# Key columns reordered by TensorE's reads instead of VectorE's writes, product turns of two engines fixed by waits, and a new written order, in a linear-attention and MLP kernel

## The chip, the cores and the metric

One core of one Trainium2 chip. The time is device microseconds (us) of one execution of the whole program; the kernel before has a median of 96.13 us over four runs.

## What is computed

Four batches b, four heads h, 1088 positions s, head size 32, sketch size r = 8:

```
a1 = S1 x, a2 = S2 x           for x = each row of q and of k      (8 numbers each)
phi(x) = outer(a1, a2)         64 numbers
kv = sum_s phi(k_s) v_s^T      (64 x 32),   z = sum_s phi(k_s)
attn_s = (phi(q_s) . kv) / (phi(q_s) . z + 1e-6)
x = attn, heads side by side   4352 tokens x 128
out = silu(x w_in) w_out       w_in 128 x 2048, w_out 2048 x 128
```

Inputs and output are float32.

## The kernel before

The MLP is cut into groups. An "h" group (L729) makes 1024 columns of x w_in in one of two double PSUM banks ("h" slots, tile H); a silu (L733, ACT) turns it into bf16 tile G; an "o" group (L746, or L743 where tokens are the rows) multiplies G by w_out and accumulates in PSUM. There are 68 groups of each kind. MLP calls are named m00, m02, m04 (batch 0), m10, m14, m20, m24 (batches 1 and 2), mR (the last 64 columns of all batches together), m30, m34, m36 (batch 3); m04h2 is the third h group of m04, m04s2 its silu, m04o2 its o group. Results leave through a transpose (tr) or copies (cp) and stores (st).

The attention for each batch feeds x to these calls. Keys: load (lk1 for batch 1), two VectorE block transposes (kt0 and kt2, function `kt`, L305) into KT, a projection on TensorE (`pairs`, L273: eight float32 matmuls of 64 x 32, one for each of two head pairs p and four column groups c), transposes back into kab (k1tr0, k1tr1, L322), products kp = outer (L328, on VectorE or GpSimd, in parts of two 32-row blocks), z (L334) and l2 (L343, L350) for the denominator's weights wm, kv (L384; in batch 0 L363), its mask copy kvm (L374, or a cast), transpose kvt (L394), copy kvc. Queries: load (lq), transposes (q1tr: L554, L622, L624), projection (L273 in batch 0, L630 after it), transposes back (L576, L581, L640, L641), then prod, red, rec, norm on VectorE (L476, L479, L482, L485), products qp = outer (L495 in batch 0, L649 after it), a transpose of qp by TensorE and a copy (pet, petc) or by DMA (dmat, L655), num (L526, L661), x copies (L163 on ACT, L165 on VectorE and GpSimd).

In KT the columns of a key block are wanted in the order of v's rows. Before, the transposes write them so: for each of four column groups c the elements land at a step of four, `(t s c)` with c innermost, and the projection reads a contiguous slice.

The order of work is not found by the compiler. Every step is a numbered task with its engine (or a choice of engines), a cost that stands only for planning, its dependencies and its slots in PSUM; the string ORDER lists all 484 tasks, "38.1" meaning task 38 on the second of its engines. `emit` walks the string and issues each task; each engine then runs its own tasks in exactly this order and waits by semaphores where data or a slot is not ready. `replay` computes planned times with the costs (it also hands out the slots); before the first h group TensorE is filled with matmuls on a zero tile (L879). SyncE issues the loads, the DMA transposes and most stores in the order of the string. A load waits until its buffer (two of each kind) is free.

The four loads of w_in and w_out halves and quarters (lwi0, lwi1, lwo0 to lwo3) come in float32 and are cast to bf16 in eight tasks cwi0 to cwi3 and cwo0 to cwo3, on GpSimd, ACT or VectorE. Task names carry the batch and first block: q0outer44 is the product of blocks 4 and 5 of batch 0's queries.

Of the kernel before, what the change touches and what calls it, by code (L numbers as in the profile page):

```python
# [16 lines left out]
0 7 22 28 23 1 29 24 2.1 25 33 3.0 30 80 32 8 34 106 31 35 38.1 11 5 40.0 36 14 37 6 55 16 50 111  # L17
48.1 56 51 18 42.0 52 58 20 26.0 59 107 53 27.0 44.0 57 108 81 109 49 110 60 39 61 43 70 46.0 152
62 82 63 9.0 153 64 41 71 65.0 47 154 45 155 4 72 54.1 66 73 156 74 84 67.0 75.1 157 85 83 114 10.1
68 86 12.0 69.0 87 76 88 244 113 77.0 15.0 247 245 89 13.0 78 198 90 115 91.0 248 250 79.1 96.1 92  # L20
116 251 259 117 246 93.1 260 118.0 123 131 262 124 97 119.0 263 125 94 98.1 253 126.0 17.2 95.0
19.0 132 254 120.0 99 133 249 21.1 134 265 112.0 100.0 136 252 266 135 274 137 261 199 275 138 277
255 139 278 264 140 280 141.0 276 281 268 279 143.1 256 142 269 159 267 283 160 282 284 286 177 161
122.0 144 287 121.0 289 163 270 290 162 257 292 206 127 167.0 293 258 271 169 128.0 295 166.0 170
129 273 285 296 130.0 205 171 145.1 147 272 288 165.0 149.1 150.0 291 200 172.0 301 164.0 201 178
202 302 203 168.0 294 179 158.0 328 180 297 181 329 331 298 207 332 182 300 304 183 330 305 184 307
299 209 333 185 308 334 186 303 335 189.0 310 306 311 313 208 190 309 187.0 314 337 336 338 210.0
223 188 316 215 317 214.0 319 146 339 211.0 216 320 322 173 323 217 340 174.0 218.0 175 312 341
176.0 213.1 343 193 191.1 344 346 196.1 204.0 342 347 195.1 349 345 101.1 350 224 315 225 382 226
348 227 383 355 228 351 356 102 385 352 384 386 103.1 388 353 229 357 230 389 148 354 358 231 387  # L30
232 359 391 192 235.0 390 392 394 237.0 318 236 151.1 233.1 395 321 361 393 238 362 364 324 212.0
365 234 367 360 368 104 370 105.1 325 363 371 373 326 396 374 397 219 327 398 400 220.0 366 401 221
376 222.0 369 377 194 240 403 197.1 243.1 399 404 436 239 437 439 241.1 402 440 242.1 442 405 443
409 406 372 410 375 408 412 378 413 407 415 379 438 416 445 381 411 446 418 380 414 419 452 417 453
421 441 422 455 444 456 424 447 425 427 448.1 449.1 420 428 451.0 430 423 431 426 450.0 468 454 469
471 429 472 458 457 459 461 432 462 474 433 460 475 477 435 463 478 470 465.1 434 473 464.1 466.1
476 467.0 479 481.1 480.0 482.1 483.0
# [9 lines left out]
class Plan:  # L47
# [3 lines left out]
    OTHER, MODE, FREE = 0.17, 0.09, 0.2  # L51
# [25 lines left out]
    def replay(self, seq):  # L77
        now, mode, queue, port = dict(self.now), None, 4.3, 0.0
        free = {k: [(i, 0.0) for i in range(len(v))] for k, v in self.slots.items()}
        for t, c in seq:  # L80
            eng, cost = t["eng"][c], t["cost"][c]
            at = max(now.get(eng, 0.0), t["ready"])
            for d in t["deps"]:
                at = max(at, d["end"] if d["dq"] and t["dq"] else d["done"] + d["lag"] + self.hop(d["on"], eng) * (d["dq"] == 0.0))
            got = []
            for pool in t["take"]:
                i, when = free[pool].pop(0)
                got.append(i)
                at = max(at, when)
            if eng == "PE":  # L90
                cost += self.MODE if mode not in (None, t["mode"]) else 0.0
                mode = t["mode"]
            if t["tt"] and eng in ("DVE", "POOL"):
                at = max(at, port)
                port = at + cost
            t["on"], t["start"], t["end"], t["got"] = eng, at, at + cost, got
            now[eng] = t["done"] = t["end"]
            if t["dq"]:
                queue = t["done"] = max(queue, t["end"]) + t["dq"]
            for u, i in t["give"]:  # L100
                free[u["take"][i]].append((u["got"][i], t["end"] + self.FREE))

    def emit(self, text, handles, fill, until):
        seq = self.order(text)
        self.replay(seq)
        last = 0.0
        for t, c in seq:
            if t["on"] == "PE":
                if last < until():
                    fill(last, min(t["start"], until()))  # L110
                last = t["end"]
            if t["fn"] is None:
                continue
            args = [self.slots[p][i] for p, i in zip(t["take"], t["got"])]
            if len(t["eng"]) > 1:
                args = [handles[t["on"]]] + args
            t["fn"](*args)
# [3 lines left out]
def kernel(  # L121
# [147 lines left out]
    def pairs(dst, srcT, lo, hi, groups=range(4)):  # L269

        for c in groups:
            for p in range(2):
                nc.tensor.matmul(dst[p][32 * c: 32 * (c + 1), lo:hi], WPf[64 * p: 64 * (p + 1), :],  # L273
                                 srcT[64 * p: 64 * (p + 1), c, lo:hi],
                                 start=True, stop=True, tile_position=(64 * p, 32 * c))

    def load(b):
        def lk():
            Kx[b] = tile_x(b, "Kx")
            load_x(nc.sync, Kx[b], k, b, 0, SA)  # L280

        def lq():
            Qx[b] = tile_x(b, "Qx")
            load_x(nc.sync, Qx[b], q, b, 0, SA)
        dk = dq = ()
        if b >= 2:
            dk, dq = ks[b - 2]["kt"], qs[b - 2]["tr"]
        at = (6.2, 24.0, 43.0)[b - 1]
        ks[b]["lk"] = dma(557, lk, dk, due=at, name=f"lk{b}")
        dv = ks[b - 2]["vcs"] if b >= 2 else []  # L290
        ks[b]["lv"] = [dma(139, lambda c=c: load_v(nc.sync, b, c), dv, due=at + 0.5, name=f"lv{b}{c}") for c in range(4)]
        qs[b]["lq"] = dma(557, lq, dq, due=at + 1.0, name=f"lq{b}")

    def key_tasks(b, cuts):
# [6 lines left out]
        def kt(c, lo, hi):  # L301
            hi = min(hi, KN[c])
            src = Kx[b][:, KA[c]: KA[c + 2], :].rearrange("p (c a) d -> p c a d", c=2)[:, :, lo:hi, :]
            dst = KT.rearrange("p q (t s c) -> p c t q s", s=8, c=4)[:, c:c + 2, lo:hi]
            nc.vector.transpose(out=dst, in_=src.rearrange("p c a d -> p c (a d)"))  # L305

        def proj0(lo, hi):
            st["p", lo] = [(H1 if lo else H0)[:, i, 0:CW] for i in range(2)]
            pairs(st["p", lo], KT, 32 * lo, 32 * hi)

        def proj(s0, s1):
            st["p", 0] = [s0, s1]
            pairs(st["p", 0], KT, 0, CW)
# [11 lines left out]
        def outer(eng, lo, hi):  # L325
            a = st["ab"][:, 0, lo:hi, :].rearrange("p a (h r) -> p (a h) r", h=H)
            bb = st["ab"][:, 1, lo:hi, :].rearrange("p a (h r) -> p (a h) r", h=H)
            eng.tensor_tensor(out=st["kp"][:, H * lo: H * hi], in0=_bc(a, 2, R), in1=_bc(bb, 1, R), op=ALU.mult)  # L328
# [75 lines left out]
        if b == 0:  # L404
            lv = [dma(139, lambda c=c: load_v(nc.sync, 0, c), due=5.0 + 0.1 * c, name=f"lv0{c}") for c in range(4)]
# [9 lines left out]
        for i, (lo, hi) in enumerate(parts):  # L415
# [6 lines left out]
            if b == 0:  # L422
                pr = pl.add("PE", 0.09 + 0.055 * (hi - lo), lambda lo=lo, hi=hi: proj0(lo, hi), k1 + [wts["WP"]] + st["pr"],
# [21 lines left out]
        tz = pl.add("PE", 0.36, z, st["tr"], take=("s",), mode="32", name=nm("z"))  # L445
# [18 lines left out]
    def scale_tasks(b, aq, mq, g0, n, deps, nm):  # L464
# [9 lines left out]
        def prod():  # L474
            alloc()
            nc.vector.tensor_tensor(out=AW[b % 2][:, g, 0:R], in0=aq(), in1=mq(), op=ALU.mult)  # L476
# [7 lines left out]
        def norm():  # L484
            nc.vector.tensor_tensor(out=st["aqs"][:, g], in0=aq(), in1=_bc(st["den"][:, g], 1, R), op=ALU.mult)  # L485
# [6 lines left out]
    def outers(b, eng, bq, lo, hi):  # L492
        st = qs[b]
        st[f"qp{lo}"] = work.tile([P, (hi - lo) * H, R, R], BF16, name="qp", tag=f"qp{lo}")
        eng.tensor_tensor(out=st[f"qp{lo}"], in0=_bc(st["aqs"][:, H * lo: H * hi], 2, R),  # L495
# [47 lines left out]
    def query_tasks(b, spans, pe=False, groups=None):  # L543
# [17 lines left out]
        def proj(s0=None, s1=None):  # L561
            st["p", lo0] = [H1[:, 0], H1[:, 1]] if first else [s0, s1]
            pairs(st["p", lo0], QT, 32 * lo0, 32 * hi0)
# [20 lines left out]
        def outer(eng, lo, hi):  # L584
            outers(b, eng, st["abm"][:, 1, lo:hi], lo, hi)
# [4 lines left out]
        pr = pl.add("PE", 0.09 + 0.058 * nn, proj, [t] + (kst["tr"][2:4] if first else []), take=() if first else ("s", "s"),  # L590
# [23 lines left out]
    def query_tasks_hm(b):  # L614
# [31 lines left out]
        def outer(eng, i):  # L646
            g0, n = (2 * NB * i, 2 * NB) if i < 2 else (H * NB, H)
            st["qp", i] = work.tile([P, n, R, R], BF16, name="qp", tag=f"hp{i}")
            eng.tensor_tensor(out=st["qp", i], in0=_bc(st["aqs"][:, g0: g0 + n], 2, R),  # L649
# [166 lines left out]
    def wq():  # L816
        for w in WQ:
            nc.gpsimd.tensor_tensor(out=w[:, 0: 2 * R].rearrange("p (n r) -> p n r", n=2), in0=WP[:, :, 0, :], in1=WP[:, :, 1, :], op=ALU.add)
# [5 lines left out]
    ld_qa = dma(262, lambda: load_x(nc.sync, Qx[0], q, 0, 0, 16), due=4.0, rate=280.0, name="lqa")  # L824
# [13 lines left out]
    for i in range(2):  # L838
        t = dma(524, lambda i=i: load_in(i), due=8.0 + 0.1 * i, rate=350.0, name=f"lwi{i}")
        win += [pl.add(("POOL", "ACT", "DVE"), (0.66, 0.6, 0.6), lambda e, w=w: cast_w(e, w_in, w_inf, w), [t], name=f"cwi{w}")  # L840
                for w in (2 * i, 2 * i + 1)]
    for i in range(4):
        t = dma(262, lambda i=i: load_out(i), due=9.0 + 0.1 * i, rate=320.0, name=f"lwo{i}")
# [8 lines left out]
    qs[0]["lq"] = dma(300, lambda: load_x(nc.sync, Qx[0], q, 0, 16, SA), due=6.0, name="lqb")  # L852
# [28 lines left out]
    pl.emit(ORDER, {"ACT": nc.scalar, "DVE": nc.vector, "POOL": nc.gpsimd, "SP": nc.sync}, fill, lambda: first_h[0]["start"])  # L881
# [30 lines left out]
```

## Time and profile before

| | |
|---|---|
| median of four runs (lowest, highest) | 96.13 us (95.72, 96.62) |
| the profiled execution | 96.6 us, span of the instructions 94.5 us |
| PE, ACT, DVE, POOL busy | 85.7, 72.9, 57.1, 37.2 us |
| first h group; last matmul ends | 16.58 us; 90.43 us |
| ACT silus | 68, 1042 ns each, next one 915 ns after the start |
| TensorE clock | full in all slices |

PE is TensorE, DVE VectorE, ACT ScalarE, POOL GpSimd, SP SyncE. A row of instructions gives start, length, engine, line, operation, what it writes and reads, its shape and how many; in brackets stands the idle time before it and who released it. In the group rows the numbers after the bar are busy us in all, mean ns of one, idle time before. A transpose or silu overlaps the next one's start, so start-to-start distances are shorter than the lengths. Before 7 us TensorE's matmuls take about double the later time per column.

### The profile page before, as it was taken

The page shows a single profiled execution, that of the slowest core. Times are in us where ns is not written, and L with a number is a line of the kernel's source. Part 1 is how long each engine was busy: PE and PEld are TensorE (multiplying, and loading weights), DVE is VectorE, ACT ScalarE, POOL GpSimd, SP SyncE. Part 2 cuts the span into 40 slices and gives each one's busy share as a digit, 9 for nine tenths or more (in the row PEclk, how much of TensorE's full clock was granted, in tenths as well). Part 3 has the DMA queues.
Part 4 walks back from the last instruction along what each step waited for, and adds up shares of the span by engine and source line. Part 5 has one row for each costly group of instructions (what it writes and reads, how often), then busy time and mean ns, then how long its engine had stood idle before and what let it go on. Part 6 is the DMA issues. An engine that isn't in the chain of part 4 may idle for free.

```text
span 94.5 us, 2456 instructions
## 1 busy us (share of the span) xinstructions
PE 85.7 (91%) x954; PEld 48.8 (52%) x954; DVE 57.1 (60%) x151; ACT 72.9 (77%) x92; POOL 37.2 (39%) x48
## 2 busy tenths in 40 slices
PE   5999758699999799999999999999999999999920
PEld 4535434567776253434453354444455667578920
DVE  5689599998789988599917389943227300202210
ACT  2335226969989795599999879999999999999810
POOL 5019508879909879900898000970000000000000
PEclk9999999999999999999999999999999999999999
DMA  1978899999961853596570003464800571010461
GB/s 34 249 240 254 239 383 401 361 326 287 274 256 31 169 96 57 134 299 111 104 146 0 7 0 59 80 132 88 139 12 0 80 116 26 20 41 2 70 125 28
DMA packets 28506, 12.93 MB, mean 137 GB/s; under 512 B 23120, under 2 KB 26704, under 8 KB 28496
## 3 DMA queue, kind: packets, MB, share of 16 engines
q1 hardware_dynamic: 28096, 12.65, 51.9%
q10 hardware_dynamic: 400, 0.14, 0.6%
q8 instruction: 7, 0.11, 0.5%
q14 instruction: 3, 0.02, 0.1%
HBM read 8.79 MB, written 2.23 MB: 117 GB/s over the span
## 4 chain that ended last, share of the span: by engine, by line
PE 64%; DVE 16%; DMA 11%; SPq 3%; issue 1%; DVEq 0%
PE H L729 29%; PE B L746 21%; DMA Kx<-in_k_dram 11%; DVE KT L305 6%; PE B L743 6%; SPq L191 2%; PE H L630 2%; DVE qabm L640 2%; PE B L273 1%; DVE qp L649 1%; PE B L661 1%; DVE QT L622 1%; DVE den L479 1%; DVE AW L476 1%; PE B L384 1%
## 5 line engine op out<-in xcount | busy, mean ns | idle before, releaser
L733 ACT ACTIVATE G<-H 128x1024 bf16<-128x1024 f32 x68 | 64.4, 1042 | 5.8 <-PE H L729 5.3
L729 PE MATMUL H<-xT,w_in 128*128 128x512 bf16 (+1 forms) x160 | 38.2, 337 | 0.0
L746 PE MATMUL B<-G,w_out 128*128 128x512 bf16 (+1 forms) x128 | 32.4, 352 | 0.0
L729 PEld LDWEIGHTS <-w_in 128*128 128x128 bf16 x176 | 18.3, 114 | 11.7 <-issue 4.2
L328 POOL TENSOR_TENSOR kp<-kab 128x512 bf16<-128x512 f32 (+1 forms) x18 | 18.3, 1041 | 11.1 <-DVE kab L322 11.1
L746 PEld LDWEIGHTS <-w_out 128*128 128x128 bf16 x128 | 12.1, 97 | 10.4 <-issue 1.2
L649 POOL TENSOR_TENSOR qp<-aqs,qabm 128x1024 bf16<-128x1024 f32 (+1 forms) x4 | 7.2, 1810 | 9.7 <-DVE aqs L485 9.7
L305 DVE STREAM_TRANSPOSE KT<-Kx 128x512 f32<-128x512 f32 (+4 forms) x10 | 9.3, 957 | 1.0 <-DMA Kx<-in_k_dram 1.0
L751 DVE STREAM_TRANSPOSE ot<-B 128x512 f32<-128x512 f32 (+1 forms) x8 | 5.1, 640 | 7.7 <-PE B L746 7.7
L879 PE MATMUL B<-zero 128*128 128x256 bf16 x36 | 8.0, 356 | 1.1 <-DVE fmask L234 1.1
L649 DVE TENSOR_TENSOR qp<-aqs,qabm 128x1024 bf16<-128x1024 f32 (+1 forms) x5 | 6.9, 1406 | 0.1
L743 PE MATMUL B<-w_out,G 128*128 128x128 bf16 x96 | 6.7, 219 | 0.0
L743 PEld LDWEIGHTS <-G 128*128 128x128 bf16 x96 | 6.0, 98 | 0.7
L165 DVE COPY ot<-B 128x128 f32<-128x128 f32 x5 | 1.3, 287 | 8.0 <-PE B L743 8.0
L879 PEld LDWEIGHTS <-zero 128*128 128x128 bf16 x36 | 4.0, 124 | 2.7 <-DVE fmask L234 1.1
L640 DVE STREAM_TRANSPOSE qabm<-H 128x256 f32<-128x256 f32 x6 | 2.6, 429 | 3.9 <-PE B L630 3.9
L165 DVE CAST xT<-B 128x512 bf16<-128x512 f32 (+1 forms) x6 | 3.7, 640 | 1.8 <-PE B L661 1.8
L495 POOL TENSOR_TENSOR qp<-aqs,qabm 128x512 bf16<-128x512 f32 (+1 forms) x3 | 3.7, 1239 | 0.4 <-DVE aqs L485 0.4
L622 DVE STREAM_TRANSPOSE QT<-Qx 128x1024 f32<-128x1024 f32 x3 | 3.7, 1223 | 0.0
L165 POOL CAST w_in<-w_inf 128x512 bf16<-128x512 f32 x3 | 2.0, 666 | 4.2 <-DMA w_inf<-in_moe_w_in_dram 4.2
L165 POOL CAST Vh<-Vf 128x1152 bf16<-128x1152 f32 x3 | 3.4, 1146 | 0.0
L273 PE MATMUL B<-KT,WP 64*32 64x288 f32 x48 | 2.2, 415 | 1.3 <-DVE KT L305 1.3
(97 smaller groups left out, 77.5 us busy)
## 6 DMA issues: line engine op xcount, KB each, us to landing
Kx<-in_k_dram SPq DMA_DIRECT2D x3, 544.0 KB, 7.3
Qx<-in_q_dram SPq DMA_DIRECT2D x3, 544.0 KB, 5.5
out_dram<-ot SPq DMA_DIRECT2D x24, 64.0 KB, 2.0
Vf<-in_v_dram SPq DMA_DIRECT2D x8, 144.0 KB, 4.4
Vf<-in_v_dram SPq DMA_DIRECT2D x8, 128.0 KB, 4.3
w_inf<-in_moe_w_in_dram SPq DMA_DIRECT2D x2, 512.0 KB, 8.3
w_outf<-in_moe_w_out_dram SPq DMA_DIRECT2D x4, 256.0 KB, 9.0
out_dram<-ot SPq DMA_DIRECT2D x16, 32.0 KB, 1.7
```

The costliest lines, as they stand in the source:

```text
L165: eng.tensor_copy(out=out, in_=in_)
L305: nc.vector.transpose(out=dst, in_=src.rearrange("p c a d -> p c (a d)"))
L328: eng.tensor_tensor(out=st["kp"][:, H * lo: H * hi], in0=_bc(a, 2, R), in1=_bc(bb, 1, R), op=ALU.mult)
L622: nc.vector.transpose(out=QT[:, :, 0: 32 * NB].rearrange("p c (a s) -> p a c s", s=32), in_=Qx[b][:, 0: 4 * NB, :].rearrange("p (a c) d -> ...
L640: nc.vector.transpose(out=dst, in_=st["p"][h][:, 0:NM])
L649: eng.tensor_tensor(out=st["qp", i], in0=_bc(st["aqs"][:, g0: g0 + n], 2, R), in1=_bc(grp(1)[:, g0: g0 + n], 1, R), op=ALU.mult)
L729: nc.tensor.matmul(view(sl, i), w_inj[:, (J * jp + i) // 4, (J * jp + i) % 4, :], x, start=True, stop=True)
L733: nc.scalar.activation(out=sl, in_=cc[jp], func=ACT.Silu)
L743: nc.tensor.matmul(d[:, 0:P], view(cc["g", jp], i)[:, P * t: P * (t + 1)], w_out[:, j, :], start=(j == 0), stop=(j == NJ - 1))
L746: nc.tensor.matmul(cc["o"][:, :n], w_out[:, j, :], view(cc["g", jp], i), start=(j == 0), stop=(j == NJ - 1))
L751: nc.vector.transpose(out=cc["ot"][:, :n], in_=cc["o"][:, :n])
L879: nc.tensor.matmul(hold["bank"][:, 0:256], zero[:, 0:P], zero, start=True, stop=True)
```

## The change

Four things. First, `kt` writes contiguously and the projection reads through a strided view, so that the columns come to PSUM in the order of before. Second, products ("tt" tasks: products with two SBUF inputs, on VectorE or GpSimd) get a wait: where the task before in the string's order of products ran on the other engine and the planned start is less than 1.5 us after its planned end, the instruction waits for that one. Third, some planning costs. Fourth, ORDER is a new string.

```
-    def pairs(dst, srcT, lo, hi, groups=range(4)):
-        for c in groups:
+    def pairs(dst, src, lo, hi):
+        for c in range(4):
             for p in range(2):
-                nc.tensor.matmul(dst[p][...], WPf[64 * p: 64 * (p + 1), :],
-                                 srcT[64 * p: 64 * (p + 1), c, lo:hi], ...
+                nc.tensor.matmul(dst[p][...], WPf[64 * p: 64 * (p + 1), :], src(p, c), ...
+    def key_cols(KT, lo, hi):
+        cols = KT.rearrange("p c (t q s) -> p q t s c", q=4, s=8)
+        return lambda p, q: cols[64 * p: 64 * (p + 1), q, lo:hi]
+    def query_cols(QT, lo, hi):
+        return lambda p, c: QT[64 * p: 64 * (p + 1), c, lo:hi]
...
-            dst = KT.rearrange("p q (t s c) -> p c t q s", s=8, c=4)[:, c:c + 2, lo:hi]
-            nc.vector.transpose(out=dst, in_=src.rearrange("p c a d -> p c (a d)"))
+            nc.vector.transpose(out=KT[:, c:c + 2, 32 * lo: 32 * hi], in_=src.rearrange("p c a d -> p c (a d)"))
...
             if t["tt"] and eng in ("DVE", "POOL"):
-                at = max(at, port)
-                port = at + cost
+                at = max(at, port + self.TURN * (user not in (None, eng)))
+                port, user = at + cost, eng
...
-            t["fn"](*args)
+            ins = t["fn"](*args)
+            if t["tt"] and t["on"] in ("DVE", "POOL"):
+                if prev and prev[0]["on"] != t["on"] and t["start"] < prev[0]["end"] + 1.5:
+                    behind(ins, prev[1])
+                prev = (t, ins)
...
+            lambda a, b: tc.add_manual_dep(getattr(a, "ins", a), getattr(b, "ins", b).name,
+                                           mybir.DependencyInfo(mybir.DependencyClass.Sync, mybir.DependencyReason.SCHED_ONLY),
+                                           reason="one port for two engines"))
```

In the new view the innermost step goes over c, 288 float32 (1152 bytes) apart. The costs changed in planning are the rates of eight loads, the batch 0 projections (0.055 to 0.11 us a block for keys, 0.058 to 0.09 for the first queries), z of batch 0 (+0.08), and a turn of 0.1 us between the engines' products.

The new order by engine, as far as it is spoken of below (task names in place of the numbers; "-" before, "+" after; the transposes of batch 0's keys keep their place):

```
PE  - m00h0 m00h1 q0num2 k1proj m00h2 q0pet4 m02h0 m00o0 k1z m02h1 q0pet6 k1l2 q0num4 m00h3 q1proj q0num6 m00o1 m02h2
PE  + m00h0 m00h1 q0num2 k1proj m02h0 q0pet4 m02h1 k1z m02h2 k1l2 q0pet6 q0num4 q1proj q0num6 m00h2 m02o0 m02o1 m04h0
PE  - ... m04h4 k2proj m04h5 m02o3 m04h6 k1kv k2z m04h7 k1kvt m04o3 k2l2 q1num m04o4 m04o5 m10h0 q2proj m04o6 m14h0 m04o7 m14h1 k3proj
PE  + ... m04h4 k1kv m04h5 k2proj k1kvt m04h6 m04o2 q1num m04h7 m04o3 k2z m14h0 m04o4 m10h0 k2l2 k3proj m14h1 m04o5 q2proj q0pet8 m14h2 m04o6 m04o7
PE  - ... m36h3 m34o3 m36o0 m36o1 m36o2 m36o3
PE  + ... m30o7 m36h3 m36o0 m36o1 m36o2 m36o3
ACT - k0vcast5 k0kvm q0petc0 cwi1 q0x0 q0petc2 m00s0 m00s1 m00s2 m02s0 k1zt
ACT + k0vcast5 cwi0 k0kvm q0petc0 q0x0 q0petc2 m00s0 q0x2 m00s1 m02s0 k1zt
DVE - q1norm q1outer0 m00tr k2kt00 k2kt20 q2tr k2tr10 k2tr00 k3kt20 m02tr k1kvm k1kvc k3kt00
DVE + q1norm q1outer1 q1outer0 k2kt20 m00tr k2kt00 m02tr k1kvm q1outer2 k2tr10 k2tr00 q1x0 k3kt00 k3kt20 q2tr
POOL - cwi0 WQ q0outer20 cwi2 cwo0 cwi3 q0outer64 k1outer0 k1outer2 cwo2 k1outer4 k1vcast q1outer1
POOL + q0outer20 cwi1 cwi2 cwi3 cwo0 q0outer64 k1outer6 k1outer2 k1outer4 k1outer8 cwo2 cwo3 k1vcast k1outer0 k2outer4
SP  - ... lq2 lk3 lv30 q1dmat0 q1dmat1 m00st0 ...       end: m30st1 m30st0 m34st1 m36st1
SP  + ... lq2 q1dmat1 q1dmat0 lk3 m00st1 m02st1 lv30 ... end: m34st0 m34st1 m30st1 m30st0 m36st0
```

## The prediction

> **What bounds the kernel now.** I read the utilisation table and the forty slices first, then the chain that ended last, then the busy time by stage, and only then the waits and single rows. The chain says what the end hangs on:
>
> ```profile
> PE 64%; DVE 16%; DMA 11%; SPq 3%; issue 1%; DVEq 0%
> PE H L729 29%; PE B L746 21%; DMA Kx<-in_k_dram 11%; DVE KT L305 6%; PE B L743 6%; SPq L191 2%; PE H L630 2%; DVE qabm L640 2%; PE B L273 1%; DVE qp L649 1%; PE B L661 1%; DVE QT L622 1%; DVE den L479 1%; DVE AW L476 1%; PE B L384 1%
> ```
>
> TensorE carries it, but the strided key transpose (L305) has 6% of it, all before 37 us. The busy time by stage (start:end, length, then PE, PEld, DVE, ACT, POOL) shows where there is room:
>
> ```profile
> 16.58:19.33 2.75, 1.90 (x29) 1.15 (x26) 2.61 (x8) 2.48 (x3) 2.08 (x4) 1.00 0.96 345
> 19.33:31.11 11.78, 11.78 (x146) 8.28 (x138) 10.66 (x26) 10.43 (x14) 9.35 (x8) 1.00 0.73 233
> 31.11:32.41 1.30, 0.81 (x17) 0.18 (x16) 1.30 (x2) 1.30 (x2) 1.30 (x3) 1.00 0.71 132
> 32.41:41.20 8.79, 8.67 (x154) 3.65 (x147) 6.92 (x20) 6.00 (x9) 6.73 (x8) 1.00 0.59 125
> 41.20:54.00 12.80, 12.78 (x150) 5.73 (x151) 8.74 (x18) 12.78 (x15) 6.21 (x6) 1.00 0.47 101
> ```
>
> TensorE is full from 19.3 us but for one hole, ACT is starved before 41 us (2.8 us idle in the fourth stage) and full after it. So time is won only by bringing matmuls, and with them silus, forward before 41 us. The waits of TensorE after the first MLP matmul name the one cause that the trace can name, and these rows show both holes:
>
> ```profile
> PE B L273 <- DVE KT L305: 1.3, 2, 0.8
> ...
> 18.68 0.72 PE L273 MATMUL B<-KT,WP 64*32 64x288 f32 x16 [0.85 <-DVE KT L305]
> ...
> 31.76 0.72 PE L273 MATMUL B<-KT,WP 64*32 64x288 f32 x16 [0.49 <-DVE KT L305]
> ```
>
> TensorE takes its instructions in the written order, so a late key transpose stops the MLP behind it.
>
> **What the Trainium skill says.** "Advanced Engine Details and Errata", SBUF Cachelines: lines are 16 bytes, two accesses to a line are needed for full speed, a new line at each access costs. The trace agrees for VectorE: L305 writes at a step of 16 bytes and takes (1216 - 477) / (576 - 192) = 1.92 ns an element, the contiguous L554 and L622 (1224 - 690) / 512 = 1.04. For TensorE's moving reads, which the change strides by 1152 bytes, no row shows it; the nearest is the weight load of w_in at a step of 8 bytes, 114 ns, beside 97 for the contiguous w_out. "SBUF — State Buffer", Who interferes with whom: a VectorE instruction with two SBUF inputs and a GpSimd instruction that reads SBUF exclude each other for the whole instruction, the later one blocks. The trace agrees:
>
> ```profile
> L649 POOL TENSOR_TENSOR qp<-aqs,qabm 128x1024 bf16<-128x1024 f32 x2 | 6.0, 2992 | 9.7 <-DVE aqs L485 9.7
> L649 DVE TENSOR_TENSOR qp<-aqs,qabm 128x256 bf16<-128x256 f32 x1 | 2.2, 2173 | 0.0
> ```
>
> GpSimd's product of 1024 would take about 2.1 us by its products of 512 (3.96 us for four), and VectorE's of 256 about 0.43 by L328; the rest, 0.9 and 1.7 us, is the other engine's turn.
>
> **The change part by part.**
>
> *Contiguous key transposes.* 512 elements: 1.10 to 0.69 us (L554). 576: 1.22 to 0.69 + 64 x 1.04 ns = 0.76. That is 0.87 us less VectorE per batch, three times. Batch 0 (320 twice, 256, 192): 0.26 twice, 0.22, 0.12, together 0.86. Of the 3.5 us in all, batch 0's is worth nothing: VectorE next waits for the second half of the queries, "QT L554 <- DMA", 1.0 us at 11.14, and that load's place in SyncE's queue is unchanged. Batch 1's loads land at 15.5; its second transpose then ends at 17.85 instead of 18.64, and the first hole shrinks. Batch 2's pair saves 0.9 us against a hole of 0.65 (31.11 to 31.76).
>
> *Strided reads in the projection.* Three in the busy part (0.65 us each from start to next start) and two in batch 0, which filler matmuls surround. Below: 0, no row speaks for a gain. Above: if TensorE pays the factor 1.92 / 1.04 = 1.85 that VectorE pays, 0.55 each. I take 0: in fp32 the 288 columns take 0.65 us where 512 bf16 columns take 0.215, so a line has some five times as long per column as in bf16. The upper end, 3 x 0.55 = 1.65, goes into the range.
>
> *Waits for the port.* The lock acts already, so a wait only fixes the turn. Cost per turn a semaphore's hop, about 0.1 us by the gaps between engines here; bounds -0.9 (a blocked product put in a better turn, row above) to +1.05 (one GpSimd product of 512 ahead of a VectorE product that could have gone first). Behind batch 1's query products stand, on VectorE, batch 2's key transposes and, on SyncE, the loads of batch 3. I take 0.
>
> *Order.* Walked by hand with the durations of the rows, a silu at 0.915 us start to start and a hop of 0.2 us. Head: cwi0 goes to ACT, in front of the mask copy k0kvm and of q0petc0. It must wait for w_in (landed at 14.15 to 14.19), so kvm slips from 12.97 to 14.7, petc0 from 14.43 to 15.1, num0 from 15.60 to 15.9, the first MLP matmul from 16.58 to 16.86: 0.28 lost. Then num2 at 17.75 and k1proj at 18.0 instead of 18.68, but the next MLP matmuls wait for ACT (x2 ends at 18.75, two silus free the H banks at 19.65 and 20.6), 0.9 us of small holes up to 23. Both orders have 12 h and 9 o groups done at 30.25 before, 30.05 after: 0.2 ahead. At batch 2's projection the transposes are done at 30.8, TensorE comes to it at 31.85: no hole. At 32.5 it has 14 h, 10 o and k1kv done, before at 32.4 13 h, 11 o and not k1kv: about 0.4 more. From there to the last o of batch 0, the old order took 8.8 us for 7.9 of work (kvx at 34.8 and the queries' transposed products, 35.9, are late). In the new one both query products of batch 1 are VectorE's, one after the other, ready at 28 and 29.2, so q1num can go at 33.5; 7.8 us for 7.6. At 40.3 it has done what the old one had at 41.2, and one h group (0.43) and pet8 (0.1) more: 1.4 us ahead; in silus 20 at 40.5 against 18 at 40.7, 1.6.
>
> *After 41 us.* ACT is full, then PE and ACT share the bound, in both orders; the lead stays. VectorE waits there and its savings are nil. At the end SyncE has four stores of m30 before the last two of m36, instead of two of m34: it ends at 1.8 us after the last matmul instead of 1.6, 0.2 lost, and half of that may lie beside ACT's stores. I book 0.1.
>
> Sum: 1.4 - 0.1 = 1.3 us. The profiled execution took 96.6 us (span 94.5 and 2.1 around it), so 95.3; that one is 0.5 above the median of 96.13, so the median becomes 94.8.
>
> **Rivals.** (1) Nothing left, 96.0. Loads of batch 3 are moved behind both query transposes of batch 1 (SyncE from 22.8 to about 30.7), and the walk has them land at 34 to 35.3, needed at 34.6. Each us by which a port turn delays the second product stops TensorE at k3proj as long. One turn of 1.05 with the 0.25 already visible eats 1.3. The same time comes from strided reads at VectorE's factor for two of the three. For it: no slack in that chain. Against it: DMA share is 0.6 to 0.7 there, the transfer takes little over 2 us once alone. (2) Slower, 97.7: TensorE's strided reads pay a full line fetch per column, 2.5 times the projection, 3 x 0.97 = 2.9 us against the gain of 1.3. It decides from 0.43 extra each (slower than before), and by over 1% from 0.75 each. For it: every column is a new line; against: the time per column in fp32. (3) More, 93.5: the lead grows after 54 us, where ACT still idles 1.3 us, and the port turns save one blocked product of 0.9. That the reads' order is wrong or the transposes stay strided I exclude: the output slice is contiguous in the new line.
>
> **Numbers.** Forecast 0.50 (own range 94.0 to 95.5), no gain 0.24, slower 0.16, more 0.10. This kernel's measurement tells about 1% from no change: faster is below 95.2, slower above 97.1. Faster 0.47 of the forecast's and 0.09 of rival 3's, 0.56; slower 0.16 and 0.02 of rival 1's, 0.18; the rest 0.26. Range: low at rival 3's 93.5, high at 97.2, through most of rival 1 and the upper bound of the strided reads.
>
> **What would show it.** KT rows of 0.69 and 0.76 us; L273 in B at 0.72 us a group (1.2 or more: rival 2); no wait of PE on KT at batch 2; first L729 at 16.9; ACT idle before 41 us reduced by 1.5 us or more; a wait of KT on DMA for batch 3 is rival 1. A shorter chain with an unchanged time would mean that the lead is given back after 54 us.

## The result and the profile after

The changed kernel takes 96.5 us (median of 36 runs) beside 96.2 us of the kernel before (55 runs) on the same chip: a ratio of 1.0015, interval 0.9995 to 1.0035. On two other chips it came out at 1.0043 [1.0000, 1.0086] and 1.0022 [0.9994, 1.0050]. So there is no gain, perhaps a loss of 0.2%; 94.8 was forecast. Ratios leave out the executions that ran visibly slower than the others of their kernel; the first profiled one of the changed kernel (97.42 us, TensorE's clock at 0.6 in two slices) was such a one, so the lines below are, with one exception, from a later profile of the same kernel, `after_third`, of 96.29 us and a span of 94.1.

The exception is the chain of the first profile, as the counterpart of the chain before; the second block is the same from `after_third`:

```profile
PE 76%; DMA 10%; ACT 4%; DVE 2%; SPq 2%; issue 1%; ACTq 0%
```

```profile
PE 71%; DMA 13%; DVE 4%; ACT 4%; SPq 3%; issue 1%; ACTq 0%; DVEq 0%
PE H L738 31%; PE B L755 25%; DMA Kx<-in_k_dram 11%; PE B L752 4%; PE B L277 4%; ACT G L742 3%; SPq L195 2%; DVE KT L314 2%; PE H L639 2%; DMA out_dram<-ot 2%; PE B L670 1%; PE B L393 1%; DVE ot L760 1%; PE B L535 1%; SPq L181 1%
```

VectorE's 16% of the chain have become 4 or 2%, L305's 6% (now L314) have become 2%, all of it before 17.4 us. In its place TensorE has 71 to 76% instead of 64, and the projection (L277, before L273) 4% instead of 1. The chain has changed just as planned, and the time has not become shorter. The groups by form, `after_third` (busy us in all, mean ns), show both sides:

```profile
L314 DVE STREAM_TRANSPOSE KT<-Kx 128x512 f32<-128x512 f32 x3 | 2.1, 694 | 0.1
L314 DVE STREAM_TRANSPOSE KT<-Kx 128x576 f32<-128x576 f32 x3 | 2.3, 759 | 0.0
L277 PE MATMUL B<-KT,WP 64*32 64x288 f32 x48 | 3.5, 652 | 0.1
L658 POOL TENSOR_TENSOR qp<-aqs,qabm 128x1024 bf16<-128x1024 f32 x2 | 3.9, 1950 | 0.0
L658 DVE TENSOR_TENSOR qp<-aqs,qabm 128x256 bf16<-128x256 f32 x2 | 0.8, 420 | 0.0
```

The transposes fell to 0.69 and 0.76 us, GpSimd's blocked product from 2992 to 1950 ns, VectorE's of 256 from 2173 to 420. But the projection's matmul, 415 ns before, has 652. The timeline has the group's place and TensorE's one hole of size left after the head:

```profile
17.41 1.18 PE L277 MATMUL B<-KT,WP 64*32 64x288 f32 x16
31.33 1.18 PE L277 MATMUL B<-KT,WP 64*32 64x288 f32 x16
...
34.15 0.41 PE L670 MATMUL B<-qt,KVd 64*32 64x512 bf16 x8 [0.62 <-ACT G L742]
...
37.38 1.18 PE L277 MATMUL B<-KT,WP 64*32 64x288 f32 x16
```

From its start to the next matmul's start a projection takes 1.11 us (31.33 to 32.44, 37.38 to 38.49, 17.41 to 18.52) instead of 0.65: 0.46 each, 1.38 in all. No transpose of keys is waited for any more at batch 2. The hole of 0.62 us is new. The page puts it down to a silu, on which the numerators (L670, q1num) do not depend; in most other profiles of the new order the same hole is put down to the DMA transpose of qp, and that is what their data comes from. The second of the two transposes of q1 settles it; first the kernel before, then `after_third`:

```profile
L655 SPq DMA_TRANSPOSE qt<-qp x1: 1231/1231/1231, 31.1 to 31.1; - x1
DMA to landing us min/median/max: 4.8/4.8/4.8
```

```profile
L664 SPq DMA_TRANSPOSE qt<-qp x1: 1276/1276/1276, 29.2 to 29.2; - x1
DMA to landing us min/median/max: 4.8/4.8/4.8
```

It is issued 1.9 us earlier than before and lands 4.8 us after its issue in both, so at 34.0 in the new order, just ahead of the numerators at 34.15.

By stage, `after_third` (columns as before):

```profile
16.03:19.98 3.95, 3.82 (x58) 2.39 (x55) 3.85 (x10) 3.54 (x5) 2.79 (x5) 1.00 1.04 375
19.98:30.78 10.80, 10.65 (x161) 7.61 (x148) 10.14 (x23) 10.02 (x14) 7.17 (x9) 1.00 0.59 177
30.78:34.15 3.37, 2.75 (x31) 0.73 (x24) 1.53 (x5) 3.03 (x4) 0.61 (x1) 1.00 0.97 233
34.15:41.30 7.15, 7.15 (x103) 2.83 (x104) 4.99 (x11) 5.02 (x9) 5.80 (x7) 1.00 0.68 156
41.30:54.00 12.70, 12.58 (x152) 5.85 (x149) 10.12 (x23) 12.11 (x14) 4.39 (x5) 1.00 0.56 109
```

TensorE's hole is in the third row (3.37 us long, 2.75 busy). From the first h group to 41.3 us ACT idles 25.27 - 21.61 = 3.7 us; before, from 16.58 to 41.2, it was 24.62 - 20.21 = 4.4.

The clearest reading is the start of the n-th silu in both profiles, counted from 0 in the timelines (us; lead is before minus after_third):

```
n                    0      5     10     14     15     20     24     27     40     67
before           17.22  23.33  29.26  34.00  35.13  42.77  46.39  49.20  62.84  88.30
after_third      16.66  23.08  28.45  33.14  35.21  42.28  45.91  49.33  62.37  88.34
lead              0.56   0.25   0.81   0.86  -0.08   0.49   0.48  -0.13   0.47  -0.04
after_reads_only 16.43  22.79  28.15  32.38  35.26  41.86  45.49  48.90  61.95  87.92
```

Of the lead, 0.56 us stands at the first silu already: w_in landed earlier in this execution, and the first h group follows the first cast of w_in by 2.4 to 2.5 us in either order (14.19 to 16.58 before, 13.53 to 16.03 here). It grows to 0.86 by the fifteenth silu and is gone at the sixteenth: there lie batch 2's projection and the hole of 0.62. The later leads of 0.49 and 0.48 are mostly a different choice of what TensorE does first: at its 25th silu the new order has issued 54 matmuls of the o groups, the old one 60. The count of weight loads (PEld, one for each matmul) of the h and o groups up to 41.2 us (before) and 41.3 us (`after_third`) shows that hardly a lead is left by then:

```profile
L729 PEld LDWEIGHTS <-w_in x56: 111/113/139, 16.5 to 41.1; 128*128 128x128 bf16 x56
L746 PEld LDWEIGHTS <-w_out x48: 95/98/100, 20.5 to 39.5; 128*128 128x128 bf16 x48
```

```profile
L738 PEld LDWEIGHTS <-w_in x56: 110/113/136, 15.9 to 40.3; 128*128 128x128 bf16 x56
L755 PEld LDWEIGHTS <-w_out x48: 96/98/98, 22.8 to 41.2; 128*128 128x128 bf16 x48
```

From the first h group to this point the new order takes 25.27 us and the old one 24.62; 1.38 of the 25.27 are the longer projections and 0.62 the hole. The last row of the table belongs to an experiment.

### The profile page after: what moved, and what is told of

The parts are those of the page before. It is cut to its first block, busy times and chain, and to the rows that moved or that the text cites. A ratio compares the mean times of both kernels' runs of the same rounds, so it can differ in the third digit from the quotient of the medians.

```text
span 95.2 us, 2461 instructions
## 1 busy us (share of the span) xinstructions
PE 87.6 (92%) x954; PEld 49.9 (52%) x954; DVE 52.5 (55%) x149; ACT 73.7 (77%) x94; POOL 32.0 (34%) x48
## 3 DMA queue, kind: packets, MB, share of 16 engines
HBM read 8.79 MB, written 2.23 MB: 116 GB/s over the span
## 4 chain that ended last, share of the span: by engine, by line
PE 76%; DMA 10%; ACT 4%; DVE 2%; SPq 2%; issue 1%; ACTq 0%
PE H L738 32%; PE B L755 25%; DMA Qx<-in_q_dram 6%; PE B L277 4%; PE B L752 4%; ACT G L742 3%; DMA Kx<-in_k_dram 3%; SPq L195 2%; PE H L639 2%; PE B L889 2%; DMA out_dram<-ot 2%; PE B L522 1%; PE B L670 1%; PE B L535 1%; PE B L393 1%; DVE ot L760 1%
## 5 line engine op out<-in xcount | busy, mean ns | idle before, releaser
L337 POOL TENSOR_TENSOR kp<-kab 128x512 bf16<-128x512 f32 (+1 forms) x18 | 16.2, 923 | 16.5 <-DVE qp L658 7.8
L889 PE MATMUL B<-zero 128*128 128x256 bf16 x36 | 8.5, 381 | 1.1 <-DVE fmask L238 1.1
L314 DVE STREAM_TRANSPOSE KT<-Kx 128x512 f32<-128x512 f32 (+4 forms) x10 | 6.1, 621 | 2.0 <-DMA Kx<-in_k_dram 1.9
L658 POOL TENSOR_TENSOR qp<-aqs,qabm 128x1024 bf16<-128x1024 f32 (+1 forms) x3 | 4.5, 1513 | 7.3 <-DVE qp L658 7.3
L658 DVE TENSOR_TENSOR qp<-aqs,qabm 128x1024 bf16<-128x1024 f32 (+1 forms) x6 | 5.6, 954 | 0.1
L504 POOL TENSOR_TENSOR qp<-aqs,qabm 128x512 bf16<-128x512 f32 (+1 forms) x3 | 2.8, 923 | 5.0 <-DVE aqs L494 4.0
L331 DVE STREAM_TRANSPOSE kab<-B 128x288 f32<-128x288 f32 x6 | 2.5, 462 | 1.8 <-PE B L277 1.8
L277 PE MATMUL B<-KT,WP 64*32 64x288 f32 x48 | 3.5, 652 | 0.0
```

What stands on the lines that cost most here:

```text
L314: nc.vector.transpose(out=KT[:, c:c + 2, 32 * lo: 32 * hi], in_=src.rearrange("p c a d -> p c (a d)"))
L337: return eng.tensor_tensor(out=st["kp"][:, H * lo: H * hi], in0=_bc(a, 2, R), in1=_bc(bb, 1, R), op=ALU.mult)
L658: return eng.tensor_tensor(out=st["qp", i], in0=_bc(st["aqs"][:, g0: g0 + n], 2, R), in1=_bc(grp(1)[:, g0: g0 + n], 1, R), op=ALU.mult)
L889: nc.tensor.matmul(hold["bank"][:, 0:256], zero[:, 0:P], zero, start=True, stop=True)
```

## The experiments

Ratios are to the kernel before on the same chip, with 95% intervals; the runs were on several chips, so between those only ratios are compared. Differences of two ratios carry about 0.4%, that is 0.4 us.

**Which part does it: parts alone and undone.** The unaltered kernel again, as a base (1.0043 [1.0000, 1.0086]):

> The changed kernel unaltered, for an undisturbed profile and as the base of the runs beside it. Both theories: 96.2 to 96.5 us, ratio to the kernel before 1.00. Theory A (the strided reads took the gain): three L277 groups of 288 columns at 1.1 us where before had 0.65, so 1.4 us more of TensorE, the stall for the key transpose gone. Theory B (the new order lost it itself): first MLP matmul 0.3 us or more later than 16.58 and new holes on TensorE of over 1 us before 41 us, whatever the projections take.

Its three groups have the 1.11 us of theory A; TensorE's new wait of 0.9 us before the numerators speaks for a part of theory B.

`after_v_blocks`: contiguous transposes and contiguous reads. The columns then come in another order, so v is loaded into 32-row blocks to match.

```
-        cols = KT.rearrange("p c (t q s) -> p q t s c", q=4, s=8)
-        return lambda p, q: cols[64 * p: 64 * (p + 1), q, lo:hi]
+        return lambda p, q: KT[64 * p: 64 * (p + 1), q, 32 * lo: 32 * hi]
...
-  Vx[b][c::4, :, 0:n]
+  Vx[b][32 * c: 32 * (c + 1), :, 0:n]
```

> The changed kernel with contiguous reads as well as contiguous key transposes: the key rows stay in blocks of 32 per column group, and the four loads of v put their rows into the same 32 partitions instead of every fourth. Theory A: the projections fall to 0.65 us, about 1.4 us of TensorE come back, 95.0 us, ratio 0.986 to before. Theory B: 96.2, within 0.4 us of the changed kernel. Both: the loads of v may land later, by up to 1.5 us each.

Measured 0.9883 [0.9854, 0.9912], 95.51 us. The group is back at 0.65 us to the next start, but the DMA issues show a side effect of the loads (KB each, us from issue to landing):

```profile
Vf<-in_v_dram SPq DMA_DIRECT2D x8, 144.0 KB, 8.1
Vf<-in_v_dram SPq DMA_DIRECT2D x8, 128.0 KB, 6.6
```

Before these were 4.4 and 4.3; SyncE on the other hand issues one in about 0.4 us instead of 0.60, w_in lands earlier (12.3 us instead of 13.5 in `after_third`), and the first h group starts at 15.12 us. The ratio is near theory A's 0.986, but this run does not isolate the reads; later ones do.

`after_strided_writes`: the new order and the waits, with the keys' old layout.

```
-            nc.vector.transpose(out=KT[:, c:c + 2, 32 * lo: 32 * hi], in_=...)
+            dst = KT.rearrange("p q (t s c) -> p c t q s", s=8, c=4)[:, c:c + 2, lo:hi]
+            nc.vector.transpose(out=dst, in_=...)
```

> The changed kernel with the key columns written at a step of four again and read contiguously: the reordering by reads undone, new order and turns kept. Theory A: 1.4 us of TensorE back, 2.6 us of VectorE lost in batches 1 to 3; the transposes of batch 2 were done 0.9 us before TensorE came to them, so about half of it is kept: 95.6. Theory B: 96.4 or more, as VectorE is slower and nothing is gained.

Measured 1.0082 [1.0041, 1.0123], 97.12 us: theory A's 95.6 was missed, and theory B's "96.4 or more" came. The waits of TensorE name two reasons:

```profile
PE B L277 <- DVE KT L314: 1.3, 1, 1.3
...
PE B L670 <- DMA qt<-qp: 1.0, 1, 1.0
```

The new order is written for the fast transposes, and has a wait on qt of its own.

`after_no_turns` (the call of `behind` left out) and `order_alone` (that and the old layout):

> The changed kernel without the waits that fix the turns of VectorE's and GpSimd's products; all else kept. Theory A: within 0.3 us of the changed kernel, products blocked by each other again (2.0 us or more for a product of 1024 elsewhere 1.95 or 1.2), none on the path. Theory B, with the turns as its cause: 0.5 us or more faster than the changed kernel.

> The new order and planning costs alone: key columns written at a step of four and read contiguously as before, no waits for turns. Theory C (the three parts add up: strided reads 1.4 us of TensorE against the relief of VectorE, turns worth 0.5, and the new order itself a loss, because batch 1's query products come late from their DMA): 1.013 times the kernel before, 97.4 us, with a wait of TensorE on qt at L670 of about 1 us. Theory D (the order is as good as the forecast's walk and was lost to the reads alone): 1.00 or below.

Measured 1.0080 [1.0052, 1.0109] and 1.0127 [1.0038, 1.0215]. Both theories on `after_no_turns` were missed: without the waits it is 0.4 to 0.65% slower than the changed kernel in its three measurements. By itself the order loses, 1.2 us at the estimate and 0.4 to 2.1 by the interval of six runs, as theory C had it. In `order_alone` TensorE waits for KT at each of the three projections:

```profile
PE B L277 <- DVE KT L314: 1.9, 3, 0.9
...
PE B L535 <- ACT qt L167: 0.7, 1, 0.7
...
PE B L670 <- DMA qt<-qp: 0.5, 1, 0.5
```

In `after_no_turns` GpSimd's small product is the blocked one (1661 ns; 623 with the waits):

```profile
L658 POOL TENSOR_TENSOR qp<-aqs,qabm 128x256 bf16<-128x256 f32 x1 | 1.7, 1661 | 4.9 <-DVE aqs L494 4.9
```

`before_strided_reads`, `before_turns` and `before_v_blocks` put one part each into the old order: contiguous writes with strided reads; the waits alone; contiguous writes and reads with v in blocks.

> The kernel before with contiguous key transposes and strided reads in the projection, its order kept and no turns. Theory C: three projections of 1.11 us instead of 0.65 cost 1.4 us, the two waits for the key transpose, 1.3 us, go or shrink: ratio 0.997 to 1.003. Theory D: the relief of VectorE is worth more than the waits that the profile names, 0.99.

> The changed kernel's code with the order of before and the key columns written at a step of four: of the change only the waits for turns and the planning costs. Theory C: the turns help here as they do in the new order, ratio 0.995. Rival: the turns are planned with an order that wasn't made for them and hold VectorE up: 1.003 or more.

> The kernel before with contiguous key transposes and contiguous reads (v's rows loaded into blocks of 32 partitions), its order kept, no turns. Theory C: the two waits for the key transpose, 1.3 us, go and nothing is paid for it: 0.985, as fast as or faster than the new order with the same layout (0.988). Theory D: the new order gains by itself, so the old one stays behind it: 0.993 or more.

Measured 0.9980 [0.9951, 1.0010], 1.0015 [0.9983, 1.0046] and 0.9935 [0.9896, 0.9974]. The first came as theory C had it; the second lies between its theory and its rival (it has the new planning costs too, which no run isolates). For the last, theory C's 0.985 was missed; its rival, D, had 0.993. In the old order the holes at the projections go and no wait on qt comes in their place. `v_blocks_no_turns` takes the waits out where the reads are contiguous:

> Contiguous transposes and reads (v in blocks) in the new order without the waits for turns. If the turns are worth their 0.5 us in this order whatever the layout: ratio to before 0.993 to 0.994, against 0.988 with them. If they only make good what slow reads did: 0.988.

0.9879 [0.9840, 0.9917], beside 0.9883 with them: no worth of theirs shows there. All of it together:

```
ratio to before         strided writes   strided reads      both contiguous, v in blocks
old order, no waits     1.000            0.998              0.9935
old order, waits        1.0015           -                  -
new order, no waits     1.0127           1.0080             0.9879
new order, waits        1.0082           1.0015 to 1.0043   0.9883
```

**The price of a strided read.** `read_steps` keeps the kernel and gives each batch's projection another walk through KT (columns in another order, so batches 1 to 3 do not compute the reference's attention): step 8 bytes, step 16, runs of 32 bytes 1152 apart.

```
+  batch 1: cols = KT.rearrange("p c (t x j) -> p c t j x", x=16, j=2)
+  batch 2: cols = KT.rearrange("p c (t x j) -> p c t j x", x=8, j=4)
+  batch 3: cols = KT.rearrange("p c (t q s) -> p q t c s", q=4, s=8)
```

> The changed kernel with other steps of the moving read in the three large projections; the columns come out in another order than v's rows, so the attention is not the reference's, the amount of work is the same. Batch 1: step 8 bytes; batch 2: step 16 bytes; batch 3: runs of 32 bytes, 1152 bytes apart. If each new 16-byte line costs and two elements of a line hide it: 0.65, 1.11, 0.65 us a group. If only far steps cost: 0.65, 0.65, and 0.65 to 0.75. If any step other than 4 bytes costs: 1.11, 1.11, 0.75.

The three groups, in order of the batches:

```profile
17.34 0.75 PE L277 MATMUL B<-KT,WP 64*32 64x288 f32 x16 [0.19 <-DVE KT L327]
...
31.88 1.23 PE L277 MATMUL B<-KT,WP 64*32 64x288 f32 x16
...
38.16 0.72 PE L277 MATMUL B<-KT,WP 64*32 64x288 f32 x16
```

Two elements of each 16-byte line suffice for nearly full speed (0.75), runs of eight are full speed (0.72, as contiguous) at 1152 bytes apart, and one element per line takes 1.23, about as much as the step of 1152 bytes (1.18). That is what the Trainium skill's "Advanced Engine Details and Errata", SBUF Cachelines, says of lines of 16 bytes and two accesses, seen here on float32 matmuls.

**Is it the loads of batch 3 (rival 1)?** `after_lk3_early` moves task lk3 in ORDER ahead of q1dmat1 and q1dmat0 in SyncE's queue; `v_blocks_lk3_early` does the same with contiguous reads.

```
SP  - q1dmat1 q1dmat0 lk3
SP  + lk3 q1dmat1 q1dmat0
```

> The changed kernel with one task moved: the load lk3 of batch 3's keys goes in front of batch 1's query transposes by DMA in SyncE's queue, where the order before had it; every other engine keeps its order. Theory C (in the new order those transposes land late because lk3 follows them at once and shares the DMA engines, and q1num comes early): the wait of TensorE on qt at L670, 0.9 us, goes or falls under 0.3, 0.5 to 0.9 us faster than the changed kernel, ratio to before 0.995. Rival: the transposes are late because their products are, the wait stays within 0.3 us, and the time within 0.2 us.

> Contiguous transposes and reads (v in blocks) in the new order with lk3 moved in front of batch 1's query transposes. Theory C: the wait on qt, 1.4 us in that kernel, falls below 0.5, ratio to before 0.978 to 0.983 against 0.988 without the move, the fastest version here. Rival: the wait stays, 0.988.

The first gives 0.9990 [0.9957, 1.0023], and the wait on qt stays at 1.0 us, as its rival said. The second, 1.0122 [1.0053, 1.0192] over six runs (the fastest took 96.86 us, beside a median of 95.51 without the move), goes against its theory: the DMA transposes, now behind lk3 and the slower v loads, took 4.81 us to issue instead of 2.7, and the wait grew from 1.4 to 3.3 us:

```profile
27.03 4.81 SPq L663 DMA_TRANSPOSE qt<-qp  x2
```

```profile
PE B L669 <- DMA qt<-qp: 3.3, 1, 3.3
```

In neither version does the wait shrink, so batch 3's key load is not what stops TensorE there. With contiguous reads it is better off behind the DMA transposes, where the change put it; with strided reads its place makes no difference that shows.

**Reads and v loads apart.** `after_reads_only` has the contiguous reads and leaves the loads of v alone; `after_v_only` has the blocks of v and leaves the strided reads. In both, keys and values no longer match, which changes the numbers and not the work.

> The changed kernel with each projection reading 32-column blocks of the key transpose contiguously; the loads of v stay as they are, so keys and values no longer match, a part of the computation that is changed here. Theory (the strided reads cost what they add in the record, three times 0.46 us): ratio to the kernel before 0.988 to 0.992, group L277 at 0.65 us from start to start. Rival (a good part of the gain of the version with blocks came from the shorter issue of its v loads, which brought w_in and the first MLP matmul forward): 0.996 to 1.000.

> The changed kernel with strided reads as it has them, but v loaded into blocks of 32 partitions; keys and values no longer match, a part of the computation that is changed here. Theory (the reads are the cost): ratio 1.000 to 1.006 to the kernel before, as the changed kernel itself, group L277 at 1.1 us. Rival (the loads bring part of the gain): 0.992 to 0.997, first MLP matmul about 0.8 us earlier than in the unaltered loads.

Measured 0.9976 [0.9940, 1.0011] and 0.9995 [0.9958, 1.0033], beside 1.0022 [0.9994, 1.0050] of the unaltered kernel (`after_third`):

> The changed kernel, unaltered, on the same chip. Both theories: ratio to the kernel before 1.000 to 1.005, as in its earlier runs.

The theory of `after_reads_only` fell. The reads are worth 0.0046 of 96.3 us, 0.45 us with an error of about 0.4, although their groups are 3 x 0.46 us shorter. Where the rest went is in the timeline of that run:

```profile
31.04 0.71 PE L277 MATMUL B<-KT,WP 64*32 64x288 f32 x16
...
32.18 0.59 PE L754 MATMUL B<-G,w_out 128*128 128x512 bf16 x2
34.20 0.41 PE L669 MATMUL B<-qt,KVd 64*32 64x512 bf16 x8 [1.42 <-DMA qt<-qp]
```

TensorE has finished the o group before the numerators at 32.8 instead of 33.5, and starts the numerators at 34.20, where the changed kernel starts them at 34.15. What it gained up to there it waits away: the silu row above leads the changed kernel by 0.76 us at the fifteenth silu and by nothing at the sixteenth. Only batch 3's projection lies behind that point: from the 21st silu to the last the lead is 0.42 us, about one projection's worth, and the measured 0.45 agrees. So in this order a lead that is there after 41 us does last to the end. The start of the numerators is set by the chain of q1 (products on VectorE, DMA transposes, numerators). SyncE issues those transposes at 27.79 in the changed kernel, at 27.63 here; the rows of SyncE's queue are, first the changed kernel's, then this one's (start, length of both issues):

```profile
27.79 2.71 SPq L664 DMA_TRANSPOSE qt<-qp  x2
```

```profile
27.63 2.71 SPq L663 DMA_TRANSPOSE qt<-qp  x2
```

The first of the two lands 3.3 us after its issue in both, the second 4.8 us in the changed kernel and 5.0 here, at 34.1. Over all nine transposes of a run the medians are 3.3 us in the new order and 2.7 in the old one, but the one that the numerators wait for is no slower than before's 4.8.

The v loads in blocks are worth about 0.3% alone (0.9995 to 1.0022, within the error, and just short of the theory's range) and 0.9% with contiguous reads (0.9883 to 0.9976); in that version all from the first h group on is 0.9 us earlier, and the DMA transposes with it, which are issued at 26.74.

**Does the wait on qt cost anything?** q1num and its two casts go two matmul groups later, behind m04h7 and m04o3:

```
PE  - m04o2 q1num m04h7 m04o3 k2z m14h0
PE  + m04o2 m04h7 m04o3 q1num k2z m14h0
```

`after_num_late2` has strided reads, `v_blocks_num_late2` contiguous ones with v in blocks, `reads_num_late` contiguous ones and v as it was (keys and values again not matching).

> The changed kernel with q1's numerators and their two casts two matmul groups later in the order (behind the h group m04h7 and the o group m04o3). Theory (the wait on the transposing DMA is a cost of the order, about 1 us of idle TensorE while it could have run those two groups): the wait of L670 on qt falls below 0.3 us and the ratio to the kernel before is 0.993 to 0.998. Rival (the wait is only moved, since the casts and the next block's h groups hang on the numerators, or ACT is full afterwards): 1.000 to 1.005.

> The same move in the version with contiguous reads and v in blocks, which waited 1.4 us on qt at this place. Theory (the wait costs): the wait falls below 0.4 us and the ratio is 0.976 to 0.983, a version faster than any before. Rival: 0.986 to 0.990, as without the move.

> Contiguous reads, loads of v untouched (keys and values do not match, a part of the computation that is changed here), q1's numerators two matmul groups later. Theory (what the strided reads cost, 1.38 us, comes through once the wait on the transposing DMA has matmuls in front of it): ratio to the kernel before 0.982 to 0.987, 1.1 us or more below the version with late numerators and strided reads (0.9975). Rival (the reads are worth only about half of what their records add, because other small waits grow as TensorE gets ahead): 0.989 to 0.994.

Measured 0.9975 [0.9947, 1.0003], 0.9846 [0.9792, 0.9901] and 0.9931 [0.9901, 0.9961]. The first is in its theory's range at the far end, 0.0047 below the unaltered kernel, about 0.45 us with an error of 0.4; the second lies between both ranges, 0.0037 below the version without the move, which its interval doesn't separate. In the second the waits read:

```profile
PE H L737 <- DVE xT L169: 0.5, 1, 0.5
...
PE B L669 <- DMA qt<-qp: 0.3, 1, 0.3
```

The move takes most of the wait on qt away and gives half a microsecond back as a wait of m14h0 on the casts of x, which follow the numerators. `reads_num_late` again gains 0.0044 over the same version with strided reads, as its rival said. In its profile the key loads land late and KT is waited for 1.1 us, so it doesn't show where the other 0.9 us goes; that the chain of q1 still sets the start of m14h0 there is argued, not shown.

`v_blocks_num_late2` has the lowest ratio of all: 94.64 us over six runs, 1.5% below the kernel before, and faster than the changed kernel; from the same layout without the move its interval does not part it.

## Why the prediction was wrong

*Contiguous transposes: right.* 0.69 and 0.76 us were forecast, 0.694 and 0.759 measured; the hole at batch 2's projection is gone and that at batch 1's too. Batch 0's part has no run of its own; VectorE's wait for the second half of the queries grew from 1.0 to 1.6 us, which fits that it is worth nothing.

*Strided reads: the term that was mis-sized.* They were priced at 0 because a float32 column takes some five times as long as a bf16 one. The upper bound, VectorE's factor of 1.85 or 0.55 us each, was the better value: 1.11 / 0.65 = 1.7, and 0.46 us each. The long time per column was no reason: `read_steps` shows that the reads of new lines are not hidden in it. With the forecast's sum this alone turns -1.3 into +0.1, that is 96.2 at the median; measured were 96.5. Rival 2's deciding point, "from 0.43 extra each", gives the right sign, but partly by luck: undone by themselves, the reads are worth only 0.45 us and not 1.38.

*That the parts add up: wrong in the sum.* The strided reads cost 1.38 us of TensorE and only 0.45 in the end, because the numerators of q1 start at 34.2 with either reads. The second step that failed is "so q1num can go at 33.5": TensorE is there at 33.5, qt lands at 34.0 and the numerators start at 34.15. With contiguous reads TensorE is there at 32.8 and the hole is 1.4. The walk had the second product ready at 29.2, and its transpose was in fact issued at 29.2; what it mis-sized is the transpose, with 4.3 us to the numerators where the landing takes 4.8. The kernel before had shown these 4.8 (31.1 to 35.9, the time that the walk itself names for "the queries' transposed products"). The walk also counted 7.9 us of work between 32.4 and 41.2 before, where its own table has TensorE busy for 8.67 of 8.79 us, so this stage seems to have had less to win than it booked. With both undone, contiguous reads and later numerators (`reads_num_late`), the ratio is 0.9931; the forecast's 94.8 is 0.986, and what takes the rest stays open.

*The lead at 41 us.* 1.4 us were forecast, 1.6 in silus; at the 21st silu it is 0.49, less than the 0.56 that were there at the first silu through w_in's landing, and in weight loads of the MLP there is none. ACT's idle time before 41 us fell by 0.7 us, not by 1.5. "The lead stays" was not put to the test by this kernel, which had none to keep; the 0.42 us of `after_reads_only` do stay.

*Head: not seen.* The 0.28 us that cwi0 on ACT should have cost aren't there: 2.4 to 2.5 us from the first cast of w_in to the first h group in both orders.

*Port waits: 0 was right for the old order and for contiguous reads* (1.0015; 0.9879 to 0.9883). In the new order with either slow layout they bring 0.4 to 0.65% (1.0127 to 1.0082, 1.0080 to 1.0015 or 1.0043); the first step is within the errors, and 1.0080 is clear of two of the changed kernel's three measurements (1.0015 and 1.0022). The rows became what the Trainium skill's "SBUF — State Buffer", Who interferes with whom, lets one expect of two engines that exclude each other, once neither waits for the other's turn: 1950 ns for GpSimd's 1024 and 420 for VectorE's 256, beside the 2.1 us and 0.43 that were worked out.

*Tail: 0.1 lost was wrong.* The last matmul ends at 90.09 us (90.42 before) with the last silu at the same time; 32 matmuls stand behind the last h group instead of 40. The span ends 4.1 us after it in both.

Rival 1 had nearly the time (96.0, and 96.5 came), and by luck, since its reason did not occur: in `after_third` k3proj does not wait for its load, and moving the load forward gave no gain that shows. Its aside, strided reads at VectorE's factor, was a part of the actual cause, together with a wait of its kind at another place: on q1's transposes, not on lk3.

What stays open: why the second transpose of q1 takes 4.8 us where the first of the changed kernel takes 3.3, what keeps `reads_num_late` from the forecast's 0.986, and how much the remaining difference between `v_blocks_num_late2` and `reads_num_late` owes to v's landing and how much to the shorter issue.

## What to carry to other kernels

A layout change moves a stride from one engine to another and doesn't remove it: price it at the reader by elements per 16-byte line, one being slow here (1.11 us instead of 0.65) and two nearly free, and take a factor measured on another engine rather than nothing. When a written order brings a consumer forward, list for it each producer's landing, the DMA's too, and compare with the time at which the engine gets there; take the landing from the very transfer in the old trace, not from a median. Time saved ahead of such a point is worth nothing unless it brings the producers forward too (as the earlier first h group of `after_v_blocks` did); time saved behind it came through nearly in full here (0.42 of 0.46 us). To see where a lead goes, set the start of the n-th instruction of one kind in both traces side by side, and count the other work that was done by then.

## What was not expected of the hardware

A float32 matmul of 64 rows and 288 columns takes 652 ns instead of 415 when each column comes from another 16-byte line, and the next group can start 1.11 instead of 0.65 us later; at a step of 8 bytes it is 424 ns. In batch 0, at 5 to 6 us, where TensorE's matmuls take about double the time per column (472 ns for 160), the same stride cost nothing: 464 and 411 ns in the first profile of the changed kernel, beside 472 and 418 before, with the contiguous query group, at 8.6 to 8.7 us, at 418 in both.

Loading v into 32 neighbouring partitions instead of every fourth made the loads land 2.3 to 3.7 us later at the median and let SyncE issue one in about 0.4 us instead of 0.60. With contiguous reads the kernel gained by it all the same (0.9883 beside 0.9976): what stands behind these loads in the queue starts earlier, w_in's first load at 5.70 us instead of 6.68.

The transpose of q1 that TensorE waits for took 4.8 us from its issue to its landing in both orders, against a median of 2.7 and 3.3 us over all transposes of the run.
